# The opening of a lightweight convolution with a cosine-gated unit: taps by quarters of the partitions, another conv tiling, another load order, slot 0 in halves

## The chip, the cores and the metric

One core of a Trainium2 chip runs the kernel. Its engines work side by side, each on its own queue of instructions: TensorE (PE, with its weight loads PEld), VectorE (DVE), ScalarE (ACT), GpSimd (POOL) and SyncE (SP), which here issues nearly all DMAs. The metric is device time in microseconds (us), the median of several runs; lower is better.

## What is computed

Per head, the seven taps are a softmax of `weight`; each token's 24 channels of that head become a causal weighted sum over itself and the six tokens before it, within a sequence. Then a feed-forward layer follows.

```
w = softmax(weight, axis=-1)                     # 8 heads x 7 taps
y[b, s, h, :] = sum_k w[h, k] * x_pad[b, s + k, h, :]   # x_pad: 6 zero rows ahead of each sequence
h = y.reshape(32768, 192) @ w_in                 # 192 -> 2048
out = (h * cos(h)) @ w_out                       # 2048 -> 192
```

x is 8 sequences of 4096 tokens with 192 channels, in float32; the kernel's products run on bf16 copies.

## The kernel before

**Units and slots.** The 32768 tokens are 32 units of 1024 (`U`, 8 blocks of 128) and 64 slots of 512 (`T`, 4 blocks). A unit is loaded and convolved as a whole and feeds two slots.

**Convolution as products.** `band` holds, for each head, a 128x256 matrix with the seven taps along its diagonals, so that a product of a block of tokens with it is the convolution (L183 `conv_mm`). The results are copied out of PSUM into `ct` (L192 `conv_out`), doubled in it by POOL (L236 `double_unit`, for the two halves of the rows of PE), and turned by a DMA transpose that SP issues (L240 `turn_unit`) into `cT`, channels on partitions. `mend_edges` (L248, POOL) mends the first six columns of each block.

**Slots.** For each slot there are eight steps j: six products `h` (`mm1`, L312, written `h0` to `h7` in the orders), the cosine on ACT and the product with it on DVE (`gcu`, L324, `s0` to `s7`), which writes `g`. `mm2_step` (L336, `m7` means seven steps) multiplies `g` by `wo` into the two banks `o_ps0` and `o_ps1`; 64 steps are one slot, `q` is the middle of a slot's 64, `p` its end. `P` and `Q` are ACT's copies of the two banks for the store. In the first 32 steps each step is one product on 64 rows; later each is a pair on the two row halves.

**The orders are written out by hand.** `PE_ORDER` and `ACT_ORDER` (L372) serve all slots from 2 on; `PE_FIRST` and `ACT_FIRST` (L375) serve slots 0 and 1. `c1`, `c2` and `d1`, `d2` are the two halves of a convolution of a coming unit (`conv_part`, L210: `c` the second or only part, `d` the first part, in slots 0 and 1 alone), `ec` and `ed` the copies out of them. Each engine takes its instructions in this order, so an instruction that waits holds up all behind it.

**Marks on SP.** `c2` may begin only after the products of `c1` have been finished; this is told through SP (class `Turn`, L154): SP waits for the products and PE waits for SP (L159 in the profile). The same is done at `q`. A mark therefore stands in SP's queue behind whatever load, store or transpose was issued ahead of it.

**PSUM.** `h` has three buffers of two banks (`h_pool`), used in turn; the convolutions take one of them (`ring_banks`) or, in slot 0, the banks `o_ps0` and `o_ps1` (`o_banks`). `x_f`, `x_bf`, `ct` and `cT` have two buffers.

**The opening (L62 to L306).** SP issues all of unit 0, `w_f`, unit 1 with its edge rows, then `wo_f`, then unit 2. ACT loads the 56 weights into one partition; one product with a column of ones spreads them over the partitions; DVE makes the softmax, then `prod` = mask x taps for all heads and taps (128x2128), four sums over the taps, and four copies put the diagonals into `band`. PE runs products on zeros (`keep_warm`, 26 of them) meanwhile. ACT and POOL cast unit 0; three engines cast the first half of `w`. `conv_first` convolves both halves of unit 0, `turn_first` turns the first half by products with `ident`, and slot 0 begins (L320). POOL then casts unit 1, doubles the second half of unit 0, casts the second half of `w`, `wo`, and so on.

Of the kernel before, what the change touches and what calls it, by code (L numbers as in the profile page):

```python
# [16 lines left out]
def kernel(  # L17
# [43 lines left out]
    w_row = consts.tile([1, H * K], FP32)  # L61
    nc.scalar.dma_start(out=w_row, in_=weight.rearrange("(o h) k -> o (h k)", o=1))  # L62
# [14 lines left out]
    load_unit(0, 0, NB)  # L77
    load_unit(0, NB, UB)
# [4 lines left out]
    for q in range(2):  # L83
        for t in range(2):
            nc.sync.dma_start(out=w_f[64 * t : 64 * t + 64, :, q * HP : (q + 1) * HP, :].rearrange("p k j f -> p k (j f)"),  # L85
                              in_=w_src[t, :, :, q * HP * 128 : (q + 1) * HP * 128])
    load_unit(1)
    wo_f = consts.tile([128, NP, 2, D], FP32)
    wo_src = moe_w_out.rearrange("(i j p) d -> p j i d", i=2, p=128)

    def load_wo(q):
        for i in range(2):
            nc.sync.dma_start(out=wo_f[:, q * HP : (q + 1) * HP, i], in_=wo_src[:, q * HP : (q + 1) * HP, i])

    load_edges(1)
    load_wo(0)
    load_wo(1)


    one = consts.tile([128, 128], FP32)  # L100
# [5 lines left out]
    def keep_warm(n):  # L106
        for _ in range(n):
            nc.tensor.matmul(out=idle, lhsT=zero[:, 0:128], rhs=zero, start=True, stop=True)  # L108

    scrap = consts.tile([128, 1], FP32)  # L110
    nc.scalar.activation(out=scrap, in_=one[:, 0:1], func=AF.Exp)  # L111
    keep_warm(3)
    w_all = o_pools[1].tile([128, T], FP32, name="o_ps1")
    w_bc = w_all[:, 0 : H * K].rearrange("p (h k) -> p h k", k=K)
    nc.tensor.matmul(out=w_all[:, 0 : H * K], lhsT=one[0:1, :], rhs=w_row, start=True, stop=True)
    keep_warm(26)
# [3 lines left out]
    nc.gpsimd.memset(xb0[:, 0, :], 0.0)  # L120

    E = 32 + K - 1
    mask = consts.tile([128, K, E], BF16)
    nc.gpsimd.memset(mask[0:32], 0.0)
    nc.gpsimd.affine_select(out=mask[0:32], in_=mask[0:32], compare_op=ALU.not_equal, fill=1.0, base=1 - K,
                            pattern=[[1, K], [1, E]], channel_multiplier=-1)
    for q in range(1, 4):
        nc.gpsimd.tensor_copy(out=mask[32 * q : 32 * q + 32], in_=mask[0:32])
    ident = consts.tile([128, 128], BF16)
# [3 lines left out]
    wn = consts.tile([128, H, K], BF16)  # L133
# [3 lines left out]
    wmax = consts.tile([128, H, 1], FP32)  # L137
    nc.vector.tensor_reduce(out=wmax[:, :, 0], in_=w_bc, axis=mybir.AxisListType.X, op=ALU.max)
    wexp = consts.tile([128, H, K], FP32)
    nc.vector.tensor_tensor(out=wexp, in0=w_bc, in1=wmax.to_broadcast([128, H, K]), op=ALU.subtract)  # L140
    nc.scalar.activation(out=wexp, in_=wexp, func=AF.Exp)
    nc.scalar.activation(out=scrap, in_=one[:, 0:1], func=AF.Sin)
    wsum = consts.tile([128, H, 1], FP32)
    nc.vector.tensor_reduce(out=wsum[:, :, 0], in_=wexp, axis=mybir.AxisListType.X, op=ALU.add)
    winv = consts.tile([128, H, 1], FP32)
    nc.vector.reciprocal(winv, wsum)
    nc.vector.tensor_tensor(out=wn, in0=wexp, in1=winv.to_broadcast([128, H, K]), op=ALU.mult)
# [20 lines left out]
    bf = {}  # L168

    def cast_unit(u, n0=0, n1=UB + 1):  # L170
        copy = nc.scalar.copy if u == 0 and n0 == 0 else nc.gpsimd.tensor_copy
        bf[u] = xb0 if u == 0 else xbf_pool.tile([128, UB + 1, D], BF16, name="x_bf")

        o = 1 if u == 0 else 0
        copy(out=bf[u][:, n0 + o : n1 + o, :].rearrange("p n (h k r) -> p (n h) k r", k=NC, r=R),  # L175
             in_=x_tiles[u][:, n0:n1, :].rearrange("p n (h r k) -> p (n h) k r", k=NC, r=R))
        if u and u % UPS == 0:
            nc.gpsimd.memset(bf[u][0:8, UB, :], 0.0)
        bf.pop(u - 2, None)
# [68 lines left out]
    def mend_edges(u):  # L248
# [3 lines left out]


    cast_unit(0, 0, NB)

    prod = consts.tile([128, K, H, E], BF16)
    nc.vector.tensor_tensor(out=prod, in0=mask.rearrange("p k (o e) -> p k o e", o=1).to_broadcast([128, K, H, E]),  # L257
                            in1=wn.rearrange("p h (k o) -> p k h o", o=1).to_broadcast([128, K, H, E]), op=ALU.mult)
    for d, n, m in ((0, 3, 3), (0, 1, 1), (2, 1, 4), (0, 1, 2)):
        nc.vector.tensor_tensor(out=prod[:, d : d + n], in0=prod[:, d : d + n], in1=prod[:, d + m : d + m + n], op=ALU.add)  # L260

    three = [nc.vector.tensor_copy, nc.scalar.copy, nc.gpsimd.tensor_copy]
    for q in range(4):
        three[q % 3](out=band[32 * q : 32 * q + 32, :, 32 * q : 32 * q + E], in_=prod[32 * q : 32 * q + 32, 0])
    cast_unit(0, NB, UB)
    for k in range(NC):
        three[(k + 2) % 3](out=w[:, k, 0:HP], in_=w_f[:, k, 0:HP])

# [4 lines left out]
    def conv_first(n0, n1):  # L273
        for c in range(2):
            ps = ring_banks()
            for i in range(4):
                for prev in range(2):
                    conv_mm(0, c, ps, i, slice(0, 128), n0 + 1 - prev, n1 + 1 - prev, prev, start=prev == 0 and i % 2 == 0, stop=prev == 1)
            yield
            for half in range(2):  # L280
                conv_out(0, c, ps, n0, n0 + 2 * half, n0 + 2 * half + 2, copies[half], double=n0 == 0)

    def turn_first(half):
        ps = h_pool.tile([128, 2, T], FP32, name="h")
        for n in range(2):
            for k in range(NC):
                nc.tensor.matmul(out=ps[:, n, k * 128 : (k + 1) * 128],
                                 lhsT=ct_tiles[0][:, 2 * half + n, k, :, :].rearrange("p t w -> p (t w)"), rhs=ident,
                                 start=True, stop=True, skip_group_check=True)
        yield  # L290
        copies[half](out=cT[0][:, 2 * half : 2 * half + 2].rearrange("p n c k -> p n (c k)"), in_=ps[:, :, 0 : NC * 128])

    list(conv_first(0, NB))
    b = conv_first(NB, UB)
    next(b)
    next(b)
    across = [turn_first(0), turn_first(1)]
    next(across[0])
    list(b)
    for half in range(2):  # L300
        list(across[half])
    cast_unit(1)
    double_unit(0, NB, UB)
    load_unit(2)
    load_edges(2)
    nc.gpsimd.tensor_copy(out=w[:, :, HP:NP], in_=w_f[:, :, HP:NP])  # L306
# [5 lines left out]
    def mm1(t, j):  # L312

        c = cT[t // TPU]
        n0 = (t % TPU) * NB
        h = h_pool.tile([128, 2, T], FP32, name="h")
        for k in range(NC):
            for i in range(2):
                rows = slice(64 * i, 64 * i + 64)
                nc.tensor.matmul(out=h[:, i, :], lhsT=w[rows, k, j, :], rhs=c[rows, n0 : n0 + NB, k, :],  # L320
# [3 lines left out]
    def gcu(t, j, h):  # L324
        cs = cos_pool.tile([128, 2, T], BF16, name="cs")
        nc.scalar.activation(out=cs, in_=h, func=AF.Sin, bias=math.pi / 2.0, scale=1.0)  # L326
        if j == 0:
            g_tiles[t] = gpool.tile([128, NF, T], BF16, name="g")
            g_tiles.pop(t - 3, None)
        nc.vector.tensor_tensor(out=g_tiles[t][:, 2 * j : 2 * j + 2, :], in0=h, in1=cs, op=ALU.mult)  # L330
# [32 lines left out]
    def store(t, b0=0, b1=2):  # L363
# [11 lines left out]
    PE_FIRST = ["h0 h1 d1 h2 d2 h3 c1 h4 c2 h5 p m8 h6 m8 h7 m4",  # L375
                "h0 m6 h1 m6 q h2 m8 h3 m4 d1 m4 d2 h4 m6 h5 c1 m6 c2 h6 h7 m4 p m8"]
    ACT_FIRST = ["s0 s1 ed1 ed2 s2 s3 ec1 ec2 s4 s5 s6 s7", "s0 s1 s2 s3 ed1 ed2 s4 s5 ec1 ec2 P s6 s7"]

    step = 0
    for t in range(NT + 2):  # L380
# [7 lines left out]
        def flush():  # L388
            while act:
# [11 lines left out]
                elif k[0] == "s" and t < NT:  # L401
                    gcu(t, int(k[1:]), h.pop(int(k[1:])))

        for k in (PE_ORDER if t > 1 else PE_FIRST[t]).split():
            if k[0] == "h" and t < NT:
                h[int(k[1:])] = mm1(t, int(k[1:]))
            elif k[0] in conv:
                next(conv[k[0]], None)
                if (t, k) == (0, "d1"):
                    turn_unit(0, NB, UB)  # L410
                    for q in range(2):
                        nc.gpsimd.tensor_copy(out=wo[:, q * HP : (q + 1) * HP], in_=wo_f[:, q * HP : (q + 1) * HP])  # L412
            elif k[0] == "m":
# [69 lines left out]
```

## Time and profile before

| what | us |
|---|---|
| median of 6 runs | 729.12 (728.14 to 729.59) |
| the profiled execution's own time | 728.41 |
| its span, from the first to the last instruction | 726.6 |
| first product of slot 0 (L320) | 14.98 |
| last product | 722.7 |

Engine idle time ahead of an instruction is given in brackets with what ended it. "SPq" and the like are the queues of an engine: time in which the engine issues a DMA or handles a semaphore. The granted clock of PE is 1.00 where it runs at full speed. A view by stretches gives the busy time of each engine between two moments; the timeline gives single instructions in order of time, those of one form behind each other on one line (`x4`).

| idle of PE in the first 50 us, by what ended it | us |
|---|---|
| products of the convolution on SP's mark (L159) | 3.8 in two waits |
| products of the convolution on POOL's cast of unit 1 (L175) | 1.9 |
| products h on DVE's g (L330) | 1.4 in three |
| the first h on DVE's copy of cT (L291) | 1.1 |

### The profile page before, as it was taken

What the parts mean: (1) busy time and instruction counts of PE and PEld (TensorE: products, weight loads), DVE (VectorE), ACT (ScalarE), POOL (GpSimd) and SP (SyncE); (2) the same over time, 40 slices, a digit from 0 to 9 for tenths busy, and PEclk for the clock granted to TensorE, in tenths of its full rate; (3) what the DMA queues carried; (4) which work ended last, traced back from release to release, by engine and by line L of the source; (5) the groups of instructions that cost most, each with busy time, mean ns of one, the idle gap of its engine ahead of it and who ended that gap; (6) DMA issues with size and microseconds to landing.
All of it is one profiled execution on the core that took longest, in us unless ns stands there. A gap on an engine that the chain in (4) does not pass through costs nothing.

```text
span 726.6 us, 26343 instructions
## 1 busy us (share of the span) xinstructions
PE 711.0 (98%) x11835; PEld 531.1 (73%) x11835; DVE 614.1 (85%) x537; ACT 617.2 (85%) x781; POOL 149.7 (21%) x119
## 2 busy tenths in 40 slices
PE   7799999999999999999999999999999999999997
PEld 3467777777777777777777777777777777777776
DVE  6768888888888888888888888888888888888984
ACT  5688888888888888888888888888988888888883
POOL 4531222201222210222211222210222211121000
PEclk9999999999999999999999999999999999999999
DMA  9844334664334554345554343555343554423411
GB/s 246 179 132 114 102 96 120 143 143 121 95 102 114 143 143 121 96 103 111 143 143 122 104 111 95 143 143 121 112 113 87 143 143 127 116 68 85 82 46 67
DMA packets 184075, 86.04 MB, mean 118 GB/s; under 512 B 111642, under 2 KB 183194, under 8 KB 183962
## 3 DMA queue, kind: packets, MB, share of 16 engines
q1 hardware_dynamic: 183960, 84.36, 44.8%
q8 instruction: 92, 1.51, 0.8%
q14 instruction: 21, 0.17, 0.1%
q10 hardware_dynamic: 2, 0.00, 0.0%
HBM read 31.36 MB, written 25.17 MB: 78 GB/s over the span
## 4 chain that ended last, share of the span: by engine, by line
PE 94%; SPq 2%; DMA 1%; DVE 1%; ACT 1%; POOL 1%; issue 0%; DVEq 0%; ACTq 0%; POOLq 0%
PE o_ps L349 46%; PE h L320 44%; PE h L186 3%; DMA wo_f<-in_moe_w_out_dram 1%; DVE g L330 1%; SPq L244 1%; ACT cs L326 1%; PE h L349 0%; SPq L85 0%; SPq L74 0%; POOL wo L412 0%; POOL w L306 0%; SPq L68 0%; DVEq L478 0%; POOL ct L238 0%
## 5 line engine op out<-in xcount | busy, mean ns | idle before, releaser
L330 DVE TENSOR_TENSOR g<-h,cs 128x1024 bf16<-128x1024 f32 x512 | 602.9, 1219 | 98.6 <-ACT cs L326 94.0
L326 ACT ACTIVATE cs<-h 128x1024 bf16<-128x1024 f32 x512 | 511.3, 1028 | 58.4 <-PE h L320 51.2
L349 PE MATMUL o_ps<-wo,g 64*128 64x192 bf16 x8128 | 424.9, 243 | 1.1 <-ACT o_sb L361 0.6
L349 PEld LDWEIGHTS <-g 64*128 64x128 bf16 x8192 | 362.4, 94 | 86.4 <-SPq L159 1.2
L320 PE MATMUL h<-cT,w 64*128 64x512 bf16 x3072 | 399.0, 376 | 2.5 <-DVE g L330 1.4
L320 PEld LDWEIGHTS <-w 64*128 64x128 bf16 x3072 | 154.5, 94 | 86.9 <-issue 3.3
L250 POOL COPY cT<-cT 128x144 bf16<-128x144 bf16 x31 | 9.5, 307 | 475.6 <-DMA cT<-ct 234.4
L201 ACT CAST ct<-h 128x432 bf16<-128x432 f32 (+1 forms) x124 | 57.2, 514 | 30.0 <-PE h L186 29.4
L175 POOL CAST x_bf<-x_f 128x1728 bf16<-128x1728 f32 (+1 forms) x32 | 80.6, 2517 | 4.2 <-DMA x_f<-in_x_dram 4.1
L361 ACT COPY o_sb<-o_ps 128x384 f32<-128x384 f32 x127 | 60.1, 473 | 6.4 <-PE o_ps L349 6.4
L238 POOL COPY ct<-ct 128x1728 bf16<-128x1728 bf16 (+1 forms) x32 | 51.3, 1602 | 46.4 <-ACT ct L201 46.4
L186 PE MATMUL h<-x_bf,band 64*128 64x216 bf16 (+1 forms) x512 | 44.9, 251 | 3.0 <-SPq L159 2.2
L186 PEld LDWEIGHTS <-band 64*128 64x128 bf16 (+1 forms) x528 | 23.1, 94 | 11.3 <-SPq L159 4.5
L108 PE MATMUL o_ps<-zero 128*128 128x512 bf16 x29 | 8.9, 472 | 1.3 <-DVE zero L103 1.3
L108 PEld LDWEIGHTS <-zero 128*128 128x128 bf16 x29 | 3.1, 114 | 5.8 <-issue 2.5
L349 PE MATMUL h<-wo,g 64*128 64x192 bf16 x64 | 5.8, 243 | 0.0
L186 PE MATMUL o_ps<-x_bf,band 64*128 64x216 bf16 x16 | 1.7, 254 | 3.6 <-POOL x_bf L175 1.9
L201 ACT CAST ct<-o_ps 128x432 bf16<-128x432 f32 x4 | 1.9, 522 | 3.0 <-PE o_ps L186 3.0
L412 POOL CAST wo<-wo_f 128x1536 bf16<-128x1536 f32 x2 | 2.9, 1470 | 0.0
L361 ACT COPY o_sb<-h 128x384 f32<-128x384 f32 x1 | 0.5, 480 | 2.4 <-PE h L349 2.4
L257 DVE TENSOR_TENSOR prod<-mask,wn 128x2128 bf16<-128x2128 bf16 x1 | 2.4, 2375 | 0.1
L111 ACT ACT_TABLE_LOAD x1 | 1.3, 1283 | 1.3 <-PEq L467 1.3
(41 smaller groups left out, 25.2 us busy)
## 6 DMA issues: line engine op xcount, KB each, us to landing
out_dram<-o_sb SPq DMA_DIRECT2D x63, 384.0 KB
x_f<-in_x_dram SPq DMA_DIRECT2D x31, 768.0 KB
x_f<-in_x_dram SPq DMA_DIRECT2D x31, 96.0 KB
w_f<-in_moe_w_in_dram SPq DMA_DIRECT2D x4, 384.0 KB
wo_f<-in_moe_w_out_dram SPq DMA_DIRECT2D x4, 384.0 KB
x_f<-in_x_dram SPq DMA_DIRECT2D x2, 384.0 KB
cT<-ct SPq DMA_TRANSPOSE x32
out_dram<-o_sb SPq DMA_DIRECT2D x2, 192.0 KB
```

The lines of the kernel that those rows point to most:

```text
L108: nc.tensor.matmul(out=idle, lhsT=zero[:, 0:128], rhs=zero, start=True, stop=True)
L175: copy(out=bf[u][:, n0 + o : n1 + o, :].rearrange("p n (h k r) -> p (n h) k r", k=NC, r=R), in_=x_tiles[u][:, n0:n1, :].rearrange("p n (h ...
L186: return nc.tensor.matmul(out=ps[i // 2][:, 0 : (n1 - n0) * 2 * G].rearrange("p (n k i r) -> p i n k r", n=n1 - n0, k=NC, i=2)[:, i % 2], ...
L201: copy(o[:, :, 0, :], i[:, :, 0, :])
L238: nc.gpsimd.tensor_copy(out=ct[:, n0:n1, :, 1, :], in_=ct[:, n0:n1, :, 0, :])
L244: nc.sync.dma_start_transpose(out=cT[u][:, n0:n1].rearrange("p n c k -> p (n c) k"), in_=ct[:, n0:n1].rearrange("p n c t k -> p (n c t k)"))
L250: nc.gpsimd.tensor_copy(out=cT[u][:, 0:UB, :, 0 : K - 1], in_=cT[u][:, UB].rearrange("p c (n t) -> p n c t", t=16)[:, :, :, 8 : 8 + K - 1])
L320: nc.tensor.matmul(out=h[:, i, :], lhsT=w[rows, k, j, :], rhs=c[rows, n0 : n0 + NB, k, :], start=(k == 0), stop=(k == NC - 1))
L326: nc.scalar.activation(out=cs, in_=h, func=AF.Sin, bias=math.pi / 2.0, scale=1.0)
L330: nc.vector.tensor_tensor(out=g_tiles[t][:, 2 * j : 2 * j + 2, :], in0=h, in1=cs, op=ALU.mult)
L349: m = nc.tensor.matmul(out=o_ps[tt, b][:, si * D : (si + 1) * D], lhsT=g_tiles[tt][rows, f, s * 128 : (s + 1) * 128], rhs=wo[rows, f // 2, ...
L361: nc.scalar.copy(o_sb[t][:, 2 * b : 2 * b + 2, :].rearrange("p s d -> p (s d)"), o_ps.pop((t, b))[:, 0 : 2 * D])
```

## The change

- **Taps.** Two heads go to each quarter of the partitions: `w_row` is 4x14, and one product with `quarter` (4x128, ones where the partition is in the quarter; POOL makes it with a memset and two selects) spreads them. The softmax, `prod` (128x532) and one reduction over the taps in place of the four sums (`diag`) work on 2 heads a partition. 16 copies, in turn on DVE, ACT and POOL, put `diag` into `band`. ACT loads the table for Sin after its cast of unit 0.
- **Loads.** The first half of `w_f` goes ahead of the second half of unit 0. `wo_f`'s four loads are issued only after POOL's cast of unit 0's second half. That cast comes after POOL's share of `w`.
- **Conv of unit 0.** `conv_first` takes two blocks and all heads per bank, on `o_ps0` and `o_ps1`, with one copy a bank; only the first half of unit 0 is convolved ahead of slot 0. The second half (`conv_rest`, key `r`) comes after `h1` in slot 0. POOL's cast of the second half of `w` comes after the doubling, as before. `turn_first` copies each block alone.
- **Slot 0** does step j = 0 in two halves of 256 tokens (`h0a`, `h0b`, `s0a`, `s0b`). The orders of slots 0 and 1 are new. 17 products on zeros in place of 26.

Slots from 2 on, and all that they call, are issued as before.

```diff
-    w_row = consts.tile([1, H * K], FP32)
+    HQ = H // 4
+    w_row = consts.tile([4, HQ * K], FP32)
...
-    load_unit(0, 0, NB)
-    load_unit(0, NB, UB)
+    load_unit(0, 0, NB)
+    load_w(0)
+    load_unit(0, NB, UB)
+    load_w(1)
     load_unit(1)
+    load_edges(1)
...
-    nc.tensor.matmul(out=w_all[:, 0 : H * K], lhsT=one[0:1, :], rhs=w_row, start=True, stop=True)
-    keep_warm(26)
+    nc.tensor.matmul(out=w_all[:, 0 : HQ * K], lhsT=quarter, rhs=w_row, start=True, stop=True)
+    keep_warm(17)
...
-    for d, n, m in ((0, 3, 3), (0, 1, 1), (2, 1, 4), (0, 1, 2)):
-        nc.vector.tensor_tensor(out=prod[:, d : d + n], in0=prod[:, d : d + n], in1=prod[:, d + m : d + m + n], op=ALU.add)
+    diag = consts.tile([128, HQ, E], FP32)
+    nc.vector.tensor_reduce(out=diag, in_=prod, axis=mybir.AxisListType.X, op=ALU.add)
...
-    for q in range(4):
-        three[q % 3](out=band[32 * q : 32 * q + 32, :, 32 * q : 32 * q + E], in_=prod[32 * q : 32 * q + 32, 0])
-    cast_unit(0, NB, UB)
+    for i in range(16):
+        q, rows = divmod(i, 4)
+        three[i % 3](out=band[32 * rows : 32 * rows + 32, HQ * q : HQ * (q + 1), 32 * rows : 32 * rows + E],
+                     in_=diag[32 * q : 32 * q + 32])
     for k in range(NC):
         three[(k + 2) % 3](out=w[:, k, 0:HP], in_=w_f[:, k, 0:HP])
+    cast_unit(0, NB, UB)
+    for q in range(2):
+        for dma in load_wo(q):
+            tc.add_manual_dep(dma.ins, bf_last[0].ins.name, sync_dep, reason="the bandwidth is for what is needed sooner")
...
+    def conv_first():
+        banks = o_banks()
+        for half in range(2):
+            for h in range(H):
+                for prev in range(2):
+                    nc.tensor.matmul(
+                        out=banks[half][:, 0 : 2 * D].rearrange("p (n k h r) -> p h n k r", n=2, k=NC, h=H)[:, h],
+                        lhsT=band[:, h, 128 * prev : 128 * prev + 128],
+                        rhs=bf[0][:, 2 * half + 1 - prev : 2 * half + 3 - prev, h * G : (h + 1) * G].rearrange(
+                            "p n (k r) -> p n k r", k=NC),
+                        start=(h == 0 and prev == 0), stop=(h == H - 1 and prev == 1), skip_group_check=True)
+            copies[half](out=ct_tiles[0][:, 2 * half : 2 * half + 2].rearrange("p n k t w -> p (n k) t w"),
+                         in_=banks[half][:, 0 : 2 * D].rearrange("p (m t w) -> p m t w", t=1, w=64).to_broadcast(
+                             [128, 2 * NC, 2, 64]))
...
+    def conv_rest():
+        banks = o_banks()
+        for c in range(2):
+            for i in range(4):
+                for prev in range(2):
+                    conv_mm(0, c, [b[:, 4 * G * 2 * c :] for b in banks], i, slice(0, 128), NB + 1 - prev, UB + 1 - prev, prev,
+                            start=c == 0 and prev == 0 and i % 2 == 0, stop=c == 1 and prev == 1 and i % 2 == 1)
+        for b in range(2):
+            for c in range(2):
+                conv_out(0, c, [x[:, 4 * G * 2 * c :] for x in banks], NB, NB, UB, copies[1 - b], banks=(b,))
...
-    PE_FIRST = ["h0 h1 d1 h2 d2 h3 c1 h4 c2 h5 p m8 h6 m8 h7 m4",
-                "h0 m6 h1 m6 q h2 m8 h3 m4 d1 m4 d2 h4 m6 h5 c1 m6 c2 h6 h7 m4 p m8"]
-    ACT_FIRST = ["s0 s1 ed1 ed2 s2 s3 ec1 ec2 s4 s5 s6 s7", "s0 s1 s2 s3 ed1 ed2 s4 s5 ec1 ec2 P s6 s7"]
+    PE_FIRST = ["h0a h0b h1 r d1 h2 d2 h3 h4 h5 h6 c1 h7 c2 p m12",
+                "h0 m8 h1 m12 q h2 h3 h4 m4 d1 m8 d2 h5 m8 h6 c1 m8 c2 h7 m4 p m8"]
+    ACT_FIRST = ["s0a s0b s1 s2 ed1 ed2 s3 s4 s5 s6 ec1 ec2 s7", "s0 s1 s2 s3 s4 ed1 ed2 s5 s6 ec1 ec2 P s7"]
```

## Prediction

> **What bounds the kernel now.** I read the page's busy times first, then the busy time of each engine by stretches, then the timeline of the first 45 us, SP's queue included. Times below are us of the profiled execution, from the start of its span.
>
> From the page, and from the answer by stretches (columns: stretch, length, then busy time with instructions of PE, PEld, DVE, ACT, POOL, then granted clock, DMA share, GB/s):
>
> ```profile
> PE 711.0 (98%) x11835; PEld 531.1 (73%) x11835; DVE 614.1 (85%) x537; ACT 617.2 (85%) x781; POOL 149.7 (21%) x119
> ```
>
> ```profile
> 14.00:18.30 4.30, 1.47 (x12) 0.69 (x13) 2.24 (x3) 2.28 (x3) 2.53 (x2) 1.00 1.10 330
> 18.30:23.10 4.80, 3.04 (x30) 1.56 (x29) 2.59 (x3) 2.79 (x4) 4.80 (x4) 1.00 1.32 277
> ...
> 35.60:44.30 8.70, 7.05 (x104) 4.66 (x105) 3.63 (x4) 6.34 (x10) 4.42 (x3) 1.00 0.33 75
> 44.30:66.00 21.70, 21.70 (x370) 16.32 (x370) 18.85 (x17) 18.99 (x25) 4.70 (x4) 1.00 0.42 115
> ```
>
> PE has no idle time from 44.30 on, and slots 2 to 63 are issued alike by both kernels. So the change is worth what it moves one event: the convolution of unit 3 in slot 2 (the product at 44.30), from which PE runs through. The timeline shows what that product stands on:
>
> ```profile
> 15.77 2.51 POOL L175 CAST x_bf<-x_f 128x1728 bf16<-128x1728 f32 x1 [4.14 <-DMA x_f<-in_x_dram]
> ...
> 18.33 0.36 PE L186 MATMUL o_ps<-x_bf,band 64*128 64x216 bf16 x4 [1.88 <-POOL x_bf L175]
> ...
> 23.12 0.36 PE L186 MATMUL o_ps<-x_bf,band 64*128 64x216 bf16 x4 [1.58 <-SPq L159]
> ...
> 30.75 4.76 SPq L244 DMA_TRANSPOSE cT<-ct  x1
> 35.62 0.36 PE L186 MATMUL h<-x_bf,band 64*128 64x216 bf16 x4 [2.23 <-SPq L159]
> ```
>
> ```profile
> 39.81 1.63 POOL L238 COPY ct<-ct 128x1728 bf16<-128x1728 bf16 x1 [1.95 <-ACT ct L201]
> ...
> 41.38 2.54 POOL L175 CAST x_bf<-x_f 128x1728 bf16<-128x1728 f32 x1
> ...
> 44.30 0.11 PEld L186 LDWEIGHTS <-band 64*128 64x128 bf16 x4 [0.35 <-DVE g L330]
> 44.30 0.36 PE L186 MATMUL h<-x_bf,band 64*128 64x216 bf16 x4
> ```
>
> The reader is to see five stations: PE stands at `d1` until POOL has cast unit 1 (18.33); at slot 0's `c2` until SP's queue is past a transpose (23.12); at slot 1's `d2` until it is past the next one (35.62); the copies of slot 1's convolution let POOL double `ct` (39.81), and POOL then casts unit 3 (ends 43.92). At 44.30 the last wait is g's, but that cast ended only 0.38 earlier.
>
> **Part by part: everything ahead of `d1`.** Quarter taps, bands, split slot 0. Sizes go by the rows 128x56 (0.216) and 128x2128 (2.375), so 0.158 + 1.04 ns an element. `prod` 128x532: 0.71 for 2.38. One reduction over 532: also 0.71 for the four sums' 1.57. Five small DVE steps lose 0.04 each. So the diagonals stand at 6.3, not 9.0. The 16 copies have no row: each is above POOL's 128x1 memset (0.11) and below the 304-element copies (0.44); I take 0.25, nearer the memset by size. ACT sets the end: x0a's bytes are moved by 3.6 (sum of GB/s slices), landing by 4.8 (w_f's first half landed 1.25 after its bytes, at 9.63), cast 1.21, Sin table 1.28 and 0.20, five copies: 8.9 instead of 9.67. The first half of w_f moves 384 KB nearer the front: 8.5. From there: ACT's w 0.62, first ct copy 0.80 (the 768-element row), three turn products, cT copies: slot 0's `h0a` at 11.65 where `h0` was at 14.98, `h1` done at 13.2, the rest of the convolution (16 products at 0.05) at 14.0. That is some 3.3 us sooner.
>
> But next in PE's queue is `d1`, and it needs unit 1's cast. SP's queue holds the same 3.24 MB up to unit 1's rows in both kernels, so that load still lands at 15.77, POOL still casts for 2.51, `d1` still runs at 18.33. The 3.3 us are paid back there: worth 0. The cover is 18.33 - 14.0 = 4.3; all 16 copies at 0.44 and a reduction at `prod`'s 2.38 would cost 2.7 of it.
>
> **wo's loads** now wait for x0b's cast (10.9). On SP, x2's loads, the marks and the transposes stand behind them. In the trace SP issued them from 6.80 to 14.60, the second alone 4.81, as if the queue were full, and x2's were through at 18.0. From 10.9 as many bytes are still ahead at each moment: I take 18.0 again. Upper end: all of it later by 4.1, 22.1, when `d1`'s mark (18.7) would be 3.4 late. Lower end: unit 1's load no longer shares with wo, and at best lands when its bytes are moved, 14.5: -1.2.
>
> **From `d1` to the end of slot 0** the new orders count. Steps from the trace: h to s 0.86, s to g 1.07, g to the h that reuses its buffer 1.28, s after s 0.92, g after g 1.18, six products h 0.65, a pair of conv copies 0.83. h2 18.52, s2 19.38, the pair ed 20.31, s3 21.13, g3 22.20, g4 23.38, h7 24.66, `c2` 25.31; its mark no longer stands behind the transpose. (h4 waits for POOL's w as before, 20.5.) Before, `c2` was at 23.12. The 1.58 stall goes, but `c2` is queued behind more. The first o product needs bank o_ps0 back from ec1: `c2` + 0.98 as before (23.12 to 24.10), so 26.29. Then m12, h0, m8, h1, m12 to `q`: 24 + 8 lone products at 0.083 and two h at 0.65: 30.26. SP's transpose starts 0.39 after the last product's start (30.36 to 30.75): **30.57, 0.18 sooner**.
>
> **Slot 1.** The same transpose, 4.76, then `d2` 0.11 on: 35.43. PE would be ready at 34.45, so it waits 1.0 instead of 2.23. From `d2` to `c2` stand two m8 for two m6 (8 products more, 0.041 each): 3.02 for 2.67, `c2` 38.45; copies end 1.40 on (38.29 to 39.69), POOL's doubling and cast as before: cast ends 44.07, PE 44.12. PE itself would be there at 42.7, since one h more is done ahead of `d2` and only s7 is left behind `P`; that gain of 1.4 waits for POOL.
>
> **Sum:** 44.12 - 44.30 = -0.2. The profiled execution took 728.41 (span 726.6 and 1.8 around it), 0.71 under the median of 729.12, which I shift: **728.9 us**.
>
> **PE's long gap.** PE has nothing from 14.0 to 18.33, 4.3 us. The longest such gap in the trace before the end is 2.23, and the six products after it still took 0.65. At the end the granted clock fell within 1 us of the last product:
>
> ```profile
> 722.00:723.00 1.00, 0.69 (x9) 0.46 (x6) 0.00 (x0) 0.28 (x1) 0.00 (x0) 1.00 0.53 177
> 723.00:724.00 1.00, 0.00 (x0) 0.00 (x0) 0.00 (x0) 0.20 (x1) 0.00 (x0) 0.75 0.00 0
> 724.00:724.50 0.50, 0.00 (x0) 0.00 (x0) 0.00 (x0) 0.00 (x0) 0.00 (x0) 0.50 0.74 253
> ```
>
> And in the first microseconds the idle products came every 0.43, from 6.72 every 0.21. Half pace after the gap is therefore possible; both ends stay: 0, or the price below. I take 0, by the 2.23 gap, the nearest row inside the kernel. [...]
>
> **Rivals.**
> - *Half pace after the gap (slower side).* h2 and h3 take 1.3 each: s2 +0.85, s3 +0.85, and h4, h5 queue behind them; `c2` comes 0.9 late, 1.3 if it lasts past 24. All later stations shift: 729.8 to 730.2. It decides if the clock falls before 18.33. For: the fall at 723.5. Against: full pace after 2.23. Chance 0.2.
> - *SP late (slower side).* wo's four issues take as long from 10.9 as they did from 6.80, so SP reaches `d1`'s mark at 22.1: `d2`, ed, s3 slip by 2.9, 731.8. It decides once SP is busy past 18.7. Against: the queue drains at the same rate. 0.07.
> - *A shorter transpose.* Its median is 3.48 of 32, and 4.76 the longest. At 3.5, PE's own order sets `d2` at 34.45: -1.2, 727.9. For: half of all are no longer than the median. Against: same place, same idle DMA. 0.15.
> - *Unit 1 lands sooner*, 0.4 to 1.2, since wo is held back: 727.7 to 728.5, and with a short transpose 727. For: the 1.25 from the last byte to the landing. Against: w_f had no wo among it up to 6.8 and the same lag. 0.18.
> - *Forecast:* 0.4, with 728.2 to 729.6 as its own range for the errors of some 30 steps.
>
> **Numbers.** About 0.2% (1.46 us) is what a measurement of this kernel can tell from none. Faster by more (under 727.66): half of the sooner landings (0.09), the short transposes that come with one or save a little more (0.06), and a tail of the forecast (0.10) for orders that overlap better than I chain them: 0.25. Slower by more (over 730.58): SP late (0.07) and half pace that lasts (0.08): 0.15. Same 0.6. Range 727.0 to 730.6: it takes in a sooner landing and half pace, and leaves SP late out.
>
> **What would show it.** h0a near 11.7 and PE idle until 18.3 before `d1`: the opening is hidden; `d1` before 17.9 refutes it. The idle after slot 0's `c2` without SP, the first o product near 26.3, the second transpose near 30.6, `d2` still ended by SP. In slot 2 the product on unit 3 ended by POOL's cast, not by g, near 44.1. Half pace would be seen in h2's six products at 1.3. If the product on unit 3 comes by 43, the chain over the doubling and the cast is misread; if unit 1's cast starts before 15.3, the load order is.

## The result: 2.4 us slower, by a load that both kernels issue

The changed kernel takes 731.12 us (median of 21 runs, 729.94 to 732.14) against 728.72 for the kernel before on the same chips (43 runs). The ratio is 1.0034 with a 95% interval of 1.0027 to 1.0041: slower, by a third of a per cent. The profiled execution took 731.96, its span 730.2.

### The profile page after: what moved, and what is told of

Read it like the earlier page. It is cut to its first block, busy times and chain, and to the rows that moved or that the text cites. A ratio compares the mean times of both kernels' runs of the same rounds, so it can differ in the third digit from the quotient of the medians.

```text
span 730.2 us, 26373 instructions
## 1 busy us (share of the span) xinstructions
PE 711.2 (97%) x11848; PEld 532.1 (73%) x11848; DVE 610.9 (84%) x535; ACT 618.0 (85%) x782; POOL 151.2 (21%) x126
## 4 chain that ended last, share of the span: by engine, by line
PE 93%; DMA 2%; POOL 1%; issue 1%; SPq 1%; ACT 0%; DVE 0%; DVEq 0%; POOLq 0%
PE o_ps L372 45%; PE h L342 44%; PE h L194 3%; DMA x_f<-in_x_dram 1%; DMA wo_f<-in_moe_w_out_dram 1%; POOL x_bf L183 1%; SPq L252 1%; PE h L372 0%; ACT cs L349 0%; POOL wo L437 0%; POOL w L435 0%; SPq L85 0%; DVE g L353 0%; DVEq L506 0%; POOL ct L246 0%
## 5 line engine op out<-in xcount | busy, mean ns | idle before, releaser
L353 DVE TENSOR_TENSOR g<-h,cs 128x1024 bf16<-128x1024 f32 (+1 forms) x513 | 603.3, 1217 | 103.2 <-ACT cs L349 98.6
L349 ACT ACTIVATE cs<-h 128x1024 bf16<-128x1024 f32 (+1 forms) x513 | 511.8, 1026 | 66.7 <-PE h L342 59.2
L342 PE MATMUL h<-cT,w 64*128 64x512 bf16 (+1 forms) x3078 | 400.5, 377 | 1.5 <-DVE g L353 0.8
L209 ACT CAST ct<-h 128x432 bf16<-128x432 f32 x120 | 56.4, 522 | 29.7 <-PE h L194 28.5
L194 PE MATMUL h<-x_bf,band 64*128 64x216 bf16 x480 | 43.0, 254 | 2.0 <-POOL x_bf L183 1.2
L194 PE MATMUL o_ps<-x_bf,band 128*128 128x96 bf16 (+1 forms) x32 | 2.7, 260 | 7.2 <-POOL x_bf L183 7.2
L110 PE MATMUL o_ps<-zero 128*128 128x512 bf16 x20 | 6.8, 506 | 1.3 <-DVE zero L105 1.3
L209 ACT CAST ct<-o_ps 128x432 bf16<-128x432 f32 (+1 forms) x6 | 2.4, 457 | 0.3 <-PE o_ps L194 0.3
```

Of the source, the lines that this page charges most:

```text
L194: return nc.tensor.matmul(out=ps[i // 2][:, 0 : (n1 - n0) * 2 * G].rearrange("p (n k i r) -> p i n k r", n=n1 - n0, k=NC, i=2)[:, i % 2], ...
L209: copy(o[:, :, 0, :], i[:, :, 0, :])
L342: nc.tensor.matmul(out=h[:, i, n0 * 128 : n1 * 128], lhsT=w[rows, k, j, :], rhs=c[rows, m0 + n0 : m0 + n1, k, :], start=(k == 0), stop=(k ...
L349: nc.scalar.activation(out=cs[:, :, part], in_=h[:, :, part], func=AF.Sin, bias=math.pi / 2.0, scale=1.0)
```

## The profile after

The timeline of POOL in the changed kernel (start, duration, instruction, idle time ahead of it and what ended it):

```profile
12.38 1.23 POOL L183 CAST x_bf<-x_f 128x768 bf16<-128x768 f32 x1 [1.56 <-DMA x_f<-in_x_dram]
19.55 2.48 POOL L183 CAST x_bf<-x_f 128x1728 bf16<-128x1728 f32 x1 [5.95 <-DMA x_f<-in_x_dram]
...
45.29 2.52 POOL L183 CAST x_bf<-x_f 128x1728 bf16<-128x1728 f32 x1
```

And that of PE:

```profile
12.54 1.52 PE L342 MATMUL h<-cT,w 64*128 64x256 bf16 x18 [0.41 <-ACT cT L310]
14.00 0.85 PE L194 MATMUL o_ps<-x_bf,band 128*128 128x96 bf16 x16
22.09 0.55 PE L194 MATMUL o_ps<-x_bf,band 64*128 64x216 bf16 x4 [7.23 <-POOL x_bf L183]
22.40 1.51 PE L342 MATMUL h<-cT,w 64*128 64x512 bf16 x6
...
29.84 0.36 PE L194 MATMUL o_ps<-x_bf,band 64*128 64x216 bf16 x4
30.82 1.00 PE L372 MATMUL o_ps<-wo,g 64*128 64x192 bf16 x10 [0.61 <-ACT ct L209]
...
39.28 0.36 PE L194 MATMUL h<-x_bf,band 64*128 64x216 bf16 x4 [0.31 <-SPq L167]
...
47.87 0.36 PE L194 MATMUL h<-x_bf,band 64*128 64x216 bf16 x4 [1.17 <-POOL x_bf L183]
```

The opening did get shorter: slot 0's first product runs at 12.54 where it ran at 14.98, and unit 0 is convolved at 14.85. Then PE has nothing for 7.23 us. POOL, idle for 5.95, waits for unit 1's rows: its cast starts at 19.55, not 15.77, so `d1` runs at 22.09 and the product on unit 3 at 47.87, 3.57 later than in before. From that product to the end of the span it is 682.3 us in both (726.6 - 44.30 and 730.2 - 47.87), and 682.1 to 682.4 in the profiles of the experiments of the table below. So everything that the change is worth lies ahead of it, and the two stretches of that are the landing of unit 1 (+3.78, cast start to cast start) and the way from there (28.53 before, 28.32 now). Of the 3.57, the medians show 2.4: this profiled execution was 0.84 above its kernel's median, that of before 0.31 below the 728.72.

Why the rows land late is in the view by stretches. Its last two columns are the busy share of the 16 DMA engines and GB/s. Before:

```profile
4.00:6.00 2.00, 2.00 (x6) 0.73 (x5) 1.60 (x4) 1.97 (x4) 0.00 (x0) 1.00 1.05 298
6.00:8.00 2.00, 2.00 (x9) 0.76 (x8) 1.97 (x2) 0.82 (x1) 0.00 (x0) 1.00 1.07 223
8.00:10.00 2.00, 2.00 (x11) 0.92 (x10) 1.85 (x7) 0.80 (x2) 0.79 (x2) 1.00 0.97 215
10.00:12.00 2.00, 1.79 (x28) 1.28 (x26) 1.44 (x3) 1.12 (x6) 1.63 (x2) 1.00 1.06 214
12.00:14.00 2.00, 1.33 (x20) 1.07 (x20) 1.74 (x9) 1.26 (x6) 0.00 (x0) 1.00 1.08 315
14.00:16.00 2.00, 1.02 (x10) 0.59 (x12) 0.83 (x1) 0.50 (x2) 0.23 (x1) 1.00 1.10 335
```

After:

```profile
4.00:6.00 2.00, 2.00 (x6) 0.76 (x5) 1.75 (x6) 0.73 (x1) 1.17 (x4) 1.00 0.91 188
6.00:8.00 2.00, 2.00 (x10) 0.86 (x9) 1.40 (x6) 1.97 (x3) 1.21 (x5) 1.00 0.94 173
8.00:10.00 2.00, 1.85 (x35) 1.20 (x33) 0.07 (x1) 1.36 (x7) 0.02 (x1) 1.00 1.06 242
10.00:12.00 2.00, 0.85 (x18) 0.71 (x14) 1.39 (x3) 1.57 (x3) 0.82 (x1) 1.00 1.07 162
12.00:14.00 2.00, 1.59 (x22) 0.76 (x19) 1.15 (x3) 1.45 (x4) 1.23 (x1) 1.00 1.09 206
14.00:16.00 2.00, 0.85 (x18) 0.70 (x16) 1.83 (x3) 1.56 (x4) 0.00 (x0) 1.00 1.11 183
```

The DMA engines are nearly as busy in both (shares of 0.97 to 1.10 before, 0.91 to 1.11 after), but a busy engine moves less. Before, x rows run at 298 to 335 GB/s and only `w_f` (6 to 12) at 214 to 223; after, everything up to 16 runs at 162 to 242. Summed from such slices, the 3.244 MB up to unit 1's edge rows are moved at 14.43 before and at 17.25 after.

The rest of the difference in landing is between the last of these bytes and the cast: 15.77 - 14.43 = 1.34 before, 19.55 - 17.25 = 2.30 after. Call this the lag.

## The experiments

All but the three full-width loads, which stand in the text, in one table. "Loads": the order of the first five loads (x0a and x0b are the two halves of unit 0). Old is x0a, x0b, the two halves of `w_f`, unit 1; new is x0a, `w_f`'s first half, x0b, its second half, unit 1. "x_f at": the byte of each partition at which the `x_f` tiles start, as the built program places them. Times of one profile each in us; medians and ratios to before over the runs.

| kernel | loads | x_f at | cast of unit 1 | product on unit 3 | median | ratio, 95% interval |
|---|---|---|---|---|---|---|
| before | old | 64,768 | 15.77 | 44.30 | 728.72 | |
| e3 orders alone | old | 64,768 | 17.07 | 45.02 | 728.31 | 0.9996, 0.9986 to 1.0006 |
| e7 wo waits | old | 64,768 | 16.46 | 43.94 | 728.24 | 0.9994, 0.9982 to 1.0005 |
| e15 before, 32 bytes on | old | 64,800 | 17.00 | 45.38 | 730.39 | 1.0022, 1.0009 to 1.0036 |
| e1 old loads | old | 61,536 | 17.48 | 45.80 | 729.92 | 1.0016, 1.0006 to 1.0027 |
| e6 old loads, wo at once | old | 61,536 | 16.95 | 45.24 | 729.48 | 1.0008, 0.9998 to 1.0018 |
| e12 opening alone | old | 61,536 | 17.80 | 46.84 | 730.81 | 1.0024, 1.0013 to 1.0034 |
| e16 e6, 32 bytes on | old | 61,568 | 18.25 | 45.71 | 729.87 | 1.0012, 1.0002 to 1.0022 |
| e2 before, new loads | new | 64,768 | 18.50 | 46.77 | 729.50 | 1.0019, 1.0009 to 1.0030 |
| e18 after, old addresses | new | 64,768 | 17.30 | 45.19 | 730.28 | 1.0025, 1.0012 to 1.0038 |
| after | new | 61,536 | 19.55 | 47.87 | 731.12 | 1.0034, 1.0027 to 1.0041 |
| e4 kept warm | new | 61,536 | 20.02 | 47.58 | 731.04 | 1.0031, 1.0017 to 1.0045 |
| e5 wo at once | new | 61,536 | 19.47 | 47.76 | 731.25 | 1.0036, 1.0022 to 1.0051 |
| e14 after, 32 bytes on | new | 61,568 | 18.23 | 46.50 | 731.20 | 1.0033, 1.0022 to 1.0044 |
| e17 unit 1 in halves | old, halves | 64,768 | 17.85 | 45.76 | 730.45 | 1.0023, 1.0011 to 1.0035 |
| e9 unit 1 first | third | 61,536 | 14.77 | 43.98 | 728.82 | 0.9999, 0.9989 to 1.0008 |
| e19 the same, r sooner | third | 64,768 | 14.86 | 41.99 | 726.41 | 0.9975, 0.9963 to 0.9988 |

**The parts of the change, one by one.** e1 gives the changed kernel the old order of `x_f` and `w_f`:

```
     load_unit(0, 0, NB)
-    load_w(0)
     load_unit(0, NB, UB)
+    load_w(0)
     load_w(1)
```

> The changed kernel with one part undone: unit 0's second half is loaded ahead of the first half of w_f again; wo's loads still wait for the cast. Theory (load order): unit 1's rows landed at 19.55 instead of 15.77 because w_f's first half now lies between the two halves of unit 0, and everything after d1 came 3.6 late. Then POOL's cast of unit 1 starts near 15.8 again, d1 near 18.3, the product on unit 3 between 44.0 and 45.0, time 728.5 to 729.6 (the upper end if PE still falls to half pace in its gap). Rival (what stands behind unit 1 or around it, wo's late issue or the earlier finish of the opening, delays the rows): the cast stays near 19.5 and the time near 731.

e2 does the reverse in the kernel before:

```
     load_unit(0, 0, NB)
-    load_unit(0, NB, UB)
...
+        if q == 0:
+            load_unit(0, NB, UB)
```

> The kernel before with one part of the change alone: w_f's first half ahead of the second half of unit 0, wo issued at once as before. Theory (load order): unit 1's cast starts near 19.5, d1 near 22, and as nothing else is new the product on unit 3 near 48: 731.5 to 732.5. Rival (wo's late issue): the cast stays near 15.8 and the time at 728.7.

e3 puts the change's orders alone into the kernel before:

```
-    PE_FIRST = ["h0 h1 d1 h2 d2 h3 c1 h4 c2 h5 p m8 h6 m8 h7 m4",
+    PE_FIRST = ["h0 h1 d1 h2 d2 h3 h4 h5 h6 c1 h7 c2 p m12",
...
-    ACT_FIRST = ["s0 s1 ed1 ed2 s2 s3 ec1 ec2 s4 s5 s6 s7", "s0 s1 s2 s3 ed1 ed2 s4 s5 ec1 ec2 P s6 s7"]
+    ACT_FIRST = ["s0 s1 s2 ed1 ed2 s3 s4 s5 s6 ec1 ec2 s7", "s0 s1 s2 s3 s4 ed1 ed2 s5 s6 ec1 ec2 P s7"]
```

> The kernel before with the new orders of slots 0 and 1 alone (slot 0's first step whole). The prediction's chain from d1 on gives -0.2: the first o product near 26.3, SP's second transpose near 30.6, the product on unit 3 ended by POOL's cast near 44.1, time 728.5 (727.5 if the second transpose is as short as the others). Rival (the orders themselves cost, c2 being queued behind more): 730 or above.

The orders are worth -0.4 with an interval that holds 0. The theory that the load order is all of it missed twice: e1 stays 0.3 above its range, with the cast at 17.48, and e2 2.0 below its own. But the load order does cost: after against e1 1.2, e2 against before 0.8 by the medians of the table and 1.4 by its ratio. The trace shows that cost early. At 1.573 MB both orders have moved the same three blocks, unit 0 and the first half of `w_f`. The nine profiles with the old order (e17 among them) are there at 7.88 to 8.58, the six with the new one at 9.01 to 9.57. Their means, 8.20 and 9.24, differ by 1.04.

**Half pace.** e4 fills PE's gap:

```
                 double_unit(0, NB, UB)
+                idle = o_pools[1].tile([128, T], FP32, name="o_ps1")
+                keep_warm(24)
```

> The changed kernel with 24 products on zeros more, on bank o_ps1 between the rest of the convolution and d1, so that PE does not stand idle from 14.9 to 22.1. Theory (half pace costs): the granted clock stays 1.00, h2's six products take 0.65 and not 1.3, slot 0's c2 comes 0.77 sooner, time 730.3. Rival (half pace lies beside ACT's and DVE's chain): same time, 731.1.

In after, PE's granted clock (third column from the end) is at half, 0.50:

```profile
18.00:20.00 2.00, 0.00 (x0) 0.00 (x0) 0.00 (x0) 0.00 (x0) 0.45 (x1) 0.98 1.11 311
20.00:22.00 2.00, 0.00 (x0) 0.00 (x0) 0.00 (x0) 0.00 (x0) 2.00 (x2) 0.50 1.10 326
...
24.00:26.00 2.00, 2.00 (x14) 0.91 (x12) 1.00 (x1) 2.00 (x4) 2.00 (x3) 0.50 1.51 211
26.00:28.00 2.00, 1.50 (x10) 0.59 (x7) 1.47 (x3) 1.86 (x3) 1.04 (x1) 0.81 0.69 150
```

With e4's products it stays whole, 1.00:

```profile
22.00:24.00 2.00, 1.43 (x18) 0.75 (x19) 0.00 (x0) 0.39 (x1) 2.00 (x3) 1.00 0.96 290
24.00:26.00 2.00, 1.42 (x14) 0.41 (x12) 1.23 (x1) 2.00 (x4) 2.00 (x2) 1.00 2.15 269
```

From `d1` to the product on unit 3 it is 25.78 in after (22.09 to 47.87) and 25.01 in e4 (22.57 to 47.58). The 0.77 is there in the one profile, but the medians, 731.04 and 731.12, don't show it; the intervals of the two ratios are wide enough to hide that much. So half pace is not what made the change 2.4 us slower: with the clock whole it still has a ratio of 1.0031. Nor is it the change's alone: the clock falls to half (0.50) in the profiles of e2, e3, e7 and e15 too, which have before's opening and a wait of 3.1 to 3.7 us ahead of `d1`, and stays whole (1.00) in that of before, with 1.88.

**wo's wait.** My next theory was that wo's held-back issue delays the landing. e5 issues wo at once in after, e6 does so in e1, e7 puts the wait into the kernel before:

```
-    for q in range(2):
-        for dma in load_wo(q):
-            tc.add_manual_dep(dma.ins, bf_last[0].ins.name, sync_dep, reason="the bandwidth is for what is needed sooner")
```

> The kernel after, with wo's four loads issued right after unit 1's edges, without the wait for x0b's cast; its load order stays. Theory W (the wait costs what the load order does not: unit 1's rows become visible late because wo's issues stand idle on SP's queue): unit 1's cast starts at 18 to 18.7, the median is 729.5 to 730.0. Rival N (something else of the new opening delays the landing by the other 1.2 to 1.6 us): the cast starts at 19 to 20 and the median stays at 730.8 to 731.4. Rival S (wo shares the DMA with unit 1): cast later than 20, 732 or more.

> The kernel after with all of before's loads: x0a, x0b, both halves of w_f, and wo at once; only the new opening (quarter taps, 16 copies, split slot 0) and the new orders of slots 0 and 1 are left. Theory W: unit 1's cast starts at 15.7 to 17.1 as with these loads in before and in the orders alone, and the median is 728.2 to 728.7. Rival N: 729.6 to 730.2, as with before's load order and the wait (729.92).

> The kernel before, with one part of the change: wo's four loads wait for the cast of x0b. Theory W: the cast of unit 1 or SP's mark behind it is late by 1.2 to 1.6, median 729.9 to 730.4. Rival N: no change, 728.4 to 729.0.

That theory fell: 731.25 without the wait in after, 728.24 with it in before. e6 has every load of before and still stands 0.8 above it by the medians (its interval just holds 1), where e3, which shares its orders, is 0.4 below. So something of the new opening seems to cost time though it issues no other load. e12 is that opening alone (e6 with before's orders):

```
-    PE_FIRST = ["h0a h0b h1 r d1 h2 d2 h3 h4 h5 h6 c1 h7 c2 p m12",
+    PE_FIRST = ["h0 h1 r d1 h2 d2 h3 c1 h4 c2 h5 p m8 h6 m8 h7 m4",
...
```

> The kernel after with all of before's loads (their order, wo at once) and before's orders of slots 0 and 1 (only the entry for the second half of unit 0's convolution stays, ahead of d1): the new opening alone. Theory N (the new opening itself costs the 0.9 to 1.2 that the kernel with old loads and new orders is above the new orders alone): median 729.6 to 730.2. Rival: the opening is hidden behind unit 1's load and worth nothing, 728.4 to 729.1; then the 1.2 between those two kernels is the scatter of the landing.

730.81: the part that was to be hidden costs 1.7 us by its ratio of 1.0024, more than either theory said.

**Addresses.** What the opening also does is shrink the constants, by 3,232 bytes in each partition, and `x_f` and all pools behind them move. e14, e15 and e16 add one unused tile to after, before and e6:

```
+    pad = consts.tile([128, 8], FP32)
```

> The kernel after with one unused tile of 32 bytes per partition at the end of the constants, and nothing else. The new opening's constants are 3,232 bytes smaller, so the tiles that the pools place behind them moved: x_f starts at byte 64,768 of each partition in before (a multiple of 64) and at 61,536 in after (32 beyond one); with the 32 bytes it is at 61,568, a multiple of 64 again. Theory A (transfers into rows that start between multiples of 64 bytes are slower, and that is what the opening costs): bytes and landing of unit 1 come 0.5 to 1.5 sooner than in after, its cast starts at 18 to 18.9, the median is 729.5 to 730.4, that of before with the new loads. Rival C (the opening's own work costs it): no change, 730.8 to 731.4.

> The kernel before with the same unused 32 bytes at the end of the constants: x_f moves from 64,768 to 64,800, 32 beyond a multiple of 64, and every pool behind it too. Not one instruction differs. Theory A: slower by 0.9 to 1.7, 729.6 to 730.5. Rival C: no change, 728.2 to 729.1.

> The kernel with the new opening and orders but all of before's loads (729.48), with the unused 32 bytes: x_f at a multiple of 64. Theory A: it comes to the level of the new orders alone, 728.0 to 728.7. Rival C: stays at 729.2 to 729.8.

Not one instruction of e15 differs from before; only `x_f` and the pools behind it start 32 bytes further on. It takes 1.7 us more by the median. In its profile the rows land later than in that of before:

```profile
17.00 2.50 POOL L175 CAST x_bf<-x_f 128x1728 bf16<-128x1728 f32 x1 [5.37 <-DMA x_f<-in_x_dram]
```

A landing in one profile proves little, since e3's cast, at before's addresses, starts at 17.07. And e14 and e16, whose rows start at a multiple of 64 again (61,568), gained nothing by their medians (though e14's cast comes 1.3 sooner than after's): 64 is not the step. No run shows a step; what the table shows is that 64,768 stands apart from the three other places. e18 therefore has after with `w_f`, `wo_f` and every tile from `x_f` on at before's bytes:

```
+    lead = consts.tile([128, 40], FP32)
...
+    pad = consts.tile([128, 768], FP32)
```

> The kernel after with two unused tiles (160 bytes behind the taps' row, 3,072 at the end of the constants), so that w_f, wo_f and every tile from x_f on start at the very bytes where before has them; no instruction differs. Theory A2 (where the transfers' destinations lie is what the opening costs, as the 32 bytes that cost before 1.8 us say, but not by multiples of 64): unit 1's cast starts at 18 to 18.9 and the median is 729.3 to 730.2, that of before with the new loads. Rival C (the opening's own work delays the landing): no change, 730.8 to 731.4.

```profile
17.30 2.48 POOL L184 CAST x_bf<-x_f 128x1728 bf16<-128x1728 f32 x1 [4.70 <-DMA x_f<-in_x_dram]
```

The cast starts 2.25 sooner than in after; the median is 0.84 less, and the two intervals overlap, so e18 alone doesn't settle it. The table does more: with the old loads, the three kernels at 64,768 lie at 728.24 to 728.72 and the five elsewhere at 729.48 to 730.81; with the new loads, the two at 64,768 at 729.50 and 730.28 and the four others at 731.04 to 731.25. No two classes of one load order overlap. Opening and placement are parted in e15 and e18 alone: e15 falls to its placement, e18 lies midway between e2 and the four.

The lag parts the profiles in the same way, without overlap. With the old loads in whole units it is 1.34 to 1.60 in the three kernels at 64,768 and 1.82 to 1.97 in the five elsewhere (e15: 17.00 - 15.18 = 1.82); with the new loads it is 1.90 and 1.84 at 64,768 and 2.21 to 2.73 elsewhere. The moments at which the bytes are moved do overlap, 14.43 to 15.55 and 15.03 to 16.28 with the old loads. So the place of the tiles is seen in how late a load counts as landed, not clearly in how fast its bytes move; why, no run shows.

At the same kind of placement (64,768 or another), no cost of the opening's own work is clear: e15 with the old one has 730.39, e12 with the new one 730.81; e18 is 0.8 above e2 by medians and 0.4 by ratios, with intervals that overlap. The new opening with the old loads at before's bytes was not run.

**Halves of the partitions.** `w_f`'s transfers write 64 partitions each. e10, e11 and e13 load its halves in after, before and e9 over all 128, one transfer for each k:

```
-        for t in range(2):
-            nc.sync.dma_start(out=w_f[64 * t : 64 * t + 64, :, q * HP : (q + 1) * HP, :].rearrange("p k j f -> p k (j f)"),
-                              in_=w_src[t, :, :, q * HP * 128 : (q + 1) * HP * 128])
+        for k in range(NC):
+            nc.sync.dma_start(out=w_f[:, k, q * HP : (q + 1) * HP, :].rearrange("p j f -> p (j f)"),
+                              in_=w_src[:, :, k, q * HP * 128 : (q + 1) * HP * 128])
```

> The kernel after with the same bytes in the same order, but each half of w_f loaded by three transfers over all 128 partitions (one for each k) where it has two over 64 partitions each. Theory P (a load to half of the partitions moves at 200 to 240 GB/s where the x rows and wo move at 320 to 370, and it drags the x rows that are queued between its parts down with it; so the new load order costs its 2.8 us of transfer): the rate stays near 320 from 4 to 12 us, 3.24 MB are moved by 12.5 to 13.5, unit 1's cast starts at 14 to 15.2, the product on unit 3 comes at 42.3 to 43.6 and the median is 726 to 727.5. Rival M (the rate falls because two streams of any kind alternate, or because of the layout of w in memory): rate and landing as in after, 730.8 to 731.4.

> The kernel before with each half of w_f loaded by three transfers over 128 partitions in place of two over 64. Theory P: the stretch of 5.4 to 12.6 us at 215 GB/s shrinks to about 4.6 us, unit 1's cast starts at 13 to 14, but here slot 0's own opening (h1 done near 16.5 in before) becomes what d1 waits for, so the median falls by 0.8 to 2.0, to 726.7 to 728. Rival M: no change, 728.4 to 729.1.

> The kernel with unit 1 ahead of w_f's second half (e9), with w_f loaded over all 128 partitions. Theory P: w_f's first half lands 2 to 3 sooner than there, slot 0's convolution is through near 13.5 in place of 16.2, unit 1's cast starts at 11 to 12.5, d1 runs at 14 to 15.5, the product on unit 3 at 40 to 41.7 and the median is 724 to 726. Rival M: as e9, 728.5 to 729.1.

All three missed, by far and alike: 753.07, 751.88 and 750.53 us, 22 to 25 us slower than before. The stretches of e10 show why:

```profile
4.00:6.00 2.00, 2.00 (x7) 0.78 (x6) 1.75 (x6) 1.69 (x2) 1.18 (x4) 1.00 0.13 51
6.00:8.00 2.00, 2.00 (x10) 0.88 (x9) 1.40 (x6) 1.91 (x6) 1.21 (x5) 1.00 0.13 51
```

A share of 0.13 is that of two engines of 16, and the transfer's outermost index, t, has two values. That the one comes from the other is not shown: no run tries another count. SP's queue then stood behind it, 4.62 and 11.62 us for the two halves' issues:

```profile
1.33 4.62 SPq L85 DMA_DIRECT2D w_f<-in_moe_w_in_dram  x3
6.00 5.08 SPq L75 DMA_DIRECT2D x_f<-in_x_dram  x1
11.13 11.62 SPq L85 DMA_DIRECT2D w_f<-in_moe_w_in_dram  x3
```

So they tell nothing of 64 partitions. e17 asks the other way round, with unit 1 of before in two halves:

```
-    load_unit(1)
+    for t in range(2):
+        nc.sync.dma_start(out=x_tiles[1][64 * t : 64 * t + 64, 0:UB, :],
+                          in_=xf[U : 2 * U, :].rearrange("(n p) d -> p n d", p=128)[64 * t : 64 * t + 64])
```

> The kernel before with unit 1's rows loaded by two transfers, over partitions 0 to 63 and 64 to 127, in place of one over 128; addresses and everything else as in before. Theory P (a load to 64 partitions moves at w_f's 200 to 240 GB/s): the 0.79 MB take 1.3 us longer than the 2.2 to 3.0 they take in before, unit 1's cast starts at 16.8 to 18.3, the median is 729.6 to 730.4. Rival M (w_f is slow for another reason): no change, 728.2 to 729.1.

730.45, just above theory P's range: the same rows cost 1.7 us more. But its rate does not show theory P at work: the 0.787 MB from 2.359 MB on took 3.44 us in e17 and 2.65 in before, but 3.50 in e3, whose rows go over 128 partitions. What stands out is the lag, 17.85 - 15.56 = 2.29. `w_f` itself had 214 to 223 GB/s in before, the x rows 298 to 335. Whether the halves are why `w_f` is slow stays open, since no run loads it in another way at a full share of the engines.

**A better version.** e9 loads x0a, x0b, `w_f`'s first half, unit 1 with its edges, and only then the second half of `w_f`, with wo at once; unit 2's loads are issued behind the first transpose:

```
     load_unit(0, 0, NB)
-    load_w(0)
     load_unit(0, NB, UB)
-    load_w(1)
+    load_w(0)
     load_unit(1)
     load_edges(1)
+    load_w(1)
...
                     turn_unit(0, NB, UB)
+                    load_unit(2)
+                    load_edges(2)
```

> The kernel after with the loads in the order x0a, x0b, w_f first half, unit 1, its edges, w_f second half, wo at once, and unit 2's loads issued behind the first transpose. If the landing of unit 1 sets the end, as the same 682.3 us from the product on unit 3 to the end in six profiles says: 0.38 MB less stand ahead of it, so it lands 1.5 to 3 sooner than in before, its cast starts at 13 to 14.3, the product on unit 3 runs at 41.3 to 43 and the median is 725.5 to 727.3. Rival (the order of loads only trades one landing for another: w_f's second half or unit 2's rows become what is late): 728.5 to 729.5, with the product on unit 3 at 44 or more though unit 1's cast starts before 14.5.

Unit 1's cast starts at 14.77, but the median is 728.82, in the rival's range: `d1` runs at 18.20, hardly sooner than before's 18.33. POOL is done at 17.3, and `d1` waits for DVE's copies of unit 0's second half, since it needs their banks. The granted clock falls to 0.50 in that wait:

```profile
15.13 0.85 PE L197 MATMUL o_ps<-x_bf,band 128*128 128x96 bf16 x16
18.20 0.54 PE L197 MATMUL o_ps<-x_bf,band 64*128 64x216 bf16 x4 [2.21 <-DVE ct L212]
```

```profile
18.00:19.00 1.00, 0.80 (x8) 0.57 (x10) 0.05 (x1) 0.00 (x0) 0.81 (x2) 0.50 1.11 330
19.00:20.00 1.00, 1.00 (x10) 0.49 (x7) 0.00 (x0) 0.00 (x0) 1.00 (x2) 0.50 1.10 326
```

e19 puts that half ahead of `h1` and the tiles at before's addresses:

```
-    PE_FIRST = ["h0a h0b h1 r d1 h2 d2 h3 h4 h5 h6 c1 h7 c2 p m12",
+    PE_FIRST = ["h0a h0b r h1 d1 h2 d2 h3 h4 h5 h6 c1 h7 c2 p m12",
```

> The kernel with unit 1 ahead of w_f's second half (e9, 728.82), at the addresses of before, and with the second half of unit 0's convolution one entry sooner (ahead of h1), since e9's d1 waited for DVE's copies of it until 18.20 while unit 1 was cast at 17.3. If that wait is what bounds e9: d1 at 17.2 to 17.5 and 0.7 to 0.9 less, 727.9 to 728.1; with theory A2 another 0.5 to 1.2 less, 726.8 to 727.5. Rival (the landing moves on its own and h1's later copies take back the gain): 728.5 to 729.2.

```profile
17.43 0.36 PE L198 MATMUL o_ps<-x_bf,band 64*128 64x216 bf16 x4 [0.48 <-POOL x_bf L187]
...
41.99 0.36 PE L198 MATMUL h<-x_bf,band 64*128 64x216 bf16 x4 [1.27 <-POOL x_bf L187]
```

`d1` runs 0.77 sooner and waits for the cast of unit 1 again, at a whole clock (1.00 from 16.2 on), and the product on unit 3 comes at 41.99. 726.41 us, ratio 0.9975 (0.9963 to 0.9988): a quarter of a per cent faster than before.

The 1.99 between the products on unit 3 of e9 and e19 are more than `d1`'s 0.77. From `d1` to `c2` it takes 7.73 in e9, with half clock, and 6.92 in e19 (25.93 and 24.35), which is 0.81; the other 0.41 come behind `c2`, where SP's second transpose takes 3.43 for 4.12. The addresses are not seen: unit 1's cast starts at 14.86 in e19 and at 14.77 in e9. What they are worth in this order was not run alone.

## Why the prediction was wrong, step by step

**The step that failed** is the one that cost the hidden opening at nothing: "SP's queue holds the same 3.24 MB up to unit 1's rows in both kernels, so that load still lands at 15.77". The bytes are the same, the landing is 19.55. Equal bytes were taken for equal time, whatever the order and the addresses. The rates of the trace of before, 214 to 223 GB/s for one kind of load and 298 to 335 for the other, warned that a load's rate is not one number; but even with a rate for each kind the sum would have been the same in both orders. Two causes stand in its place: the order of the loads (0.8 to 1.4 by medians and ratios, 1.04 of it seen at 1.573 MB) and the place of the tiles (0.8 to 1.7: after beside e18 and e2, e15 beside before, e1 and e6 beside e3; of these only e15 and e18 differ in the place alone). Less the 0.4 of the orders, their sum of 1.2 to 2.7 holds the 2.4; that they simply add up is assumed, since no run undoes both in the changed kernel. Not shown is why the same three blocks take 1.04 longer in one order; a part is that the engines' share falls to 0.91 and 0.94 between 4 and 8 us of after, where before has 1.05 and 1.07.

**15.77 itself was early.** Of the nine profiles with the old loads it is the earliest; the other two at before's addresses with unit 1 in one load, e3 and e7, have 17.07 and 16.46, and the kernel before alone ran from 726.99 to 731.17. A landing read from one profile needs that much room, and the range gave it 1.2 to the sooner side and nothing to the later. The whole clock of that profile was no rule either: of 135 executions of before beside the experiments, the 53 with a mean granted clock of 0.998 or more took 727.00 to 729.28 and the 35 with 0.994 or less 729.17 to 731.74. A later landing and a longer gap of PE would give both; no run of before parts them.

**The lag was read too short.** The prediction takes 1.25 us from the last byte of `w_f`'s first half to its landing at 9.63. By the slices its bytes are moved at 7.88, which makes 1.75. In after, unit 0's first half is cast from 5.27 on, 1.76 after its bytes (3.51), not from 4.8.

**The rival "unit 1 lands sooner"** had the right place and the wrong sign. **SP late** did come about in part: SP was through with unit 2's loads at 21.74, near the 22.1 of the upper end, not at the 18.0 that was taken; it cost nothing, because `d1` itself came at 22.09.

**From `d1` on, the chain was right**: 25.78 from `d1` to the product on unit 3, for 44.12 - 18.33 = 25.79 forecast. Two errors cancel in it. Half pace, which was priced at 0.9 to 1.3 and given a chance of 0.2, happened: `c2` came 7.75 after `d1`, not 6.98 (6.92 in e4, where the clock is whole). And the transpose behind `q` was shorter, by 4.76 - 4.08 = 0.68. The forecast of -0.2 for the orders agrees with e3's -0.4, whose interval holds 0 as well.

**The opening's own steps** were nearly right: `prod` 0.47 (0.71 forecast), the reduction 0.71 (0.71), the copies 0.26 to 0.29 each on the three engines (0.25). `h0a` came at 12.54 for 11.65, since the first half of `w_f` landed at 9.92, not 8.5, by the same misjudged rate.

**Chances.** Slower had 0.15, all of it for half pace and SP. Half pace came, but keeping the clock whole (e4) gave nothing that the medians show; SP cost nothing. For a later landing there was no chance at all.

## What to carry to other kernels

A load's landing is not its bytes divided by the rate of its neighbours (here the same 3.24 MB let the cast start at 15.77 in one kernel and at 19.55 in the other): read each kind's own rate and the lag behind its last byte from the stretches, of more than one profile, and when the order of the loads changes, give the range room to both sides. When a change adds or drops a small tile, look at where the big tiles behind it begin; 32 unused bytes cost this kernel 1.7 us. And before shortening a stage, ask which load ends the wait behind it, move that load first, and then look for the wait that is next.

## What the runs showed of the hardware

- Moving the `x_f` tiles and all pools behind them by 32 bytes made the same program 1.0022 times as long (1.0009 to 1.0036).
- From the last byte of unit 1's load to the cast that waits for it, 1.34 to 1.60 us passed where the `x_f` tiles start at byte 64,768, and 1.82 to 1.97 where they start at 61,536, 61,568 or 64,800 (old loads, eight profiles).
- A load of `w_f` over 128 partitions whose outermost index had two values moved 51 GB/s at a share of 0.13, for 214 to 223 as two transfers of 64 partitions.
- In after, the granted clock fell to 0.50 at 19.9, 5.1 us after the last product (14.85); in e3 it fell 2.7 us after one (15.9 to 18.7) and in e9 2.0 us (16.0 to 18.0). The half clock lasted until about 26.8 in after.
